# Cluster attention and two expert layers on one core: fp32r transposes of queries, keys and third weights, first loads on two queues, the last output chunk in halves

## The chip, the cores and the metric

The kernel runs on one core of a Trainium2 chip. TensorE (PE, with its weight loads, PEld), VectorE (DVE), ScalarE (ACT) and GpSimd (POOL) each run their own instructions in order and wait for each other by semaphores; SyncE (SP) issues most of the DMAs. The metric is device microseconds of one execution. Before the change the median of three runs is 740.92 us (740.73 to 741.88).

## The reference

```python
B, H, S, D = 2, 8, 768, 64          # 16 heads in all, 16 centroids a head
q_assign = argmax(q_n . c_n)         # each query and key goes to its nearest centroid
k_assign = argmax(k_n . c_n)
scores = q @ k.T / 8, -1e9 where q_assign != k_assign
x = softmax(scores) @ v              # to 1536 tokens x 512
x = ((x @ w1) * (x @ w2)) @ w3 @ w_out          # w1, w2: 512x1024; w3: 1024x1024; w_out: 1024x512
h = x @ w_in2                                   # 512x2048
out = (h * clip(h + 3, 0, 6) / 6) @ w_out2      # 2048x512
```

The weights of the two expert layers come as 64-bit floats and are read as pairs of 32-bit words.

## The kernel before, in words

**Order.** Every piece of work is an `op` with a key, an engine, the keys it needs and the buffer rings it takes and drops. `Plan.order` (L333) sorts the ops by the table `RANK`, which holds one place in the whole program for each op, and picks the engine of an op with a choice from the strings in `ON`. The ops are then emitted in that order, and each engine runs its own in that order. Nothing is scheduled at run time.

**Attention, about the first 350 us.** For each of the 16 heads (`prep_ops`, L684) SP loads the queries and keys side by side into `qkn`, 128 tokens x 6 chunks x 128 columns (`load_qk`, L581, each a 192 KB DMA). PE transposes the six 128x128 chunks in two groups of three (`qk_T`, L605, tile `ptqk`), against the fp32 identity `id_f`. ACT writes the rounded half `qkH`, DVE the remainder `qkL`; SP moves parts between partitions (`kk`). PE multiplies by the centroids (`pa`), nine steps on DVE and POOL (`oh0` to `oh8`) make codes of the nearest centroid, and these enter the scores as 16 extra rows. Then for each of six chunks: scores on PE (tile `pst`, L746), row maximum on DVE (tile `den`, L758), exponential on ACT (tile `p`, L780). PE transposes `p` in groups of four (tile `ptr`, L796), ACT and DVE split the result in two fp32r halves `ph` and `pl`, PE multiplies by the values (`av`, L820).

The transposes of `p` are already in fp32r. `p` is written as an fp32 tile; `p_raw` (L764) then takes a second tile `praw` of type fp32r in the same buffer, with a pad of eight columns more, and writes one column of the pad from the constant `three`. The transposes read the data through `praw` and wait for that small write.

**Weights, beside attention.** Each 512 KB piece of 64-bit weights is loaded to `raw` and turned into fp32 by five ops (`conv_ops`, L994): two on ACT (`cvt`, `cvs`), a clamp on POOL or DVE (L1008), two on DVE (L1017, L1021). The result is in `cvs`, a ring of three buffers. `w3` is transposed on PE in 16 groups of four (`w3_T`, L1037, tile `pt`), again against `id_f`, and multiplied by `w_out` (`psw`, L1068), so that the layer needs one product less per token.

**After attention**, PE runs the products of the first layer for the first batch (L1144) beside attention, then the rest (`psab`, `psx`), and then the second layer (`psh`, L1707, and `po`, L1751). At the very end each of six 128x512 chunks of the output is copied from PSUM by ACT (`out_copy`, L1756) and stored by SP (`out_store`, L1760).

**Start.** SP issues all first loads. ACT loads the table of the square root for the centroids (`root`), and later that of the exponential (`warm`). PE has four blocks of matmuls without use (`idle`, L530) between its first real work.

Of the kernel before, what the change touches and what calls it, by code (L numbers as in the profile page):

```python
# [1858 lines left out]
```

## Time and profile before

| | |
|---|---|
| median of three runs | 740.92 us |
| the profiled execution's own time | 741.47 us |
| its span, first to last instruction | 739.7 us |
| busy: PE, DVE, ACT, POOL | 719.0, 611.5, 546.8, 201.9 us |
| matmuls | 4143 |

The span is taken from the first to the last instruction of the profile. Busy time of PE counts overlapping matmuls once. The prediction reads PE from the times at which its matmuls start, since a matmul's own duration overlaps the next one.

### The profile page before, as it was taken

The numbers are of one execution on the slowest core, as the hardware profiler recorded it, in microseconds if no ns is written. First come the engines' busy times: TensorE is split into PE (matmuls) and PEld (weight loads), VectorE is DVE, ScalarE is ACT, GpSimd is POOL, SyncE is SP. The second block draws the span as 40 slices with busy tenths as digits, with TensorE's granted clock in tenths as the row PEclk, the third lists the DMA queues.
The fourth block names the chain that finished last, engine by engine and source line by source line (L and its number), as shares of the span: only waits on it lengthen the run. The fifth ranks groups of instructions, "written<-read, shape, count | busy, mean of one in ns | idle before, by whom it ended". The sixth has DMA issues, their size and how long they took to land. (4 is left out here: it accounts for less than half of the span.)

```text
span 739.7 us, 12102 instructions
## 1 busy us (share of the span) xinstructions
PE 719.0 (97%) x4143; PEld 661.4 (89%) x4143; DVE 611.5 (83%) x1060; ACT 546.8 (74%) x1043; POOL 201.9 (27%) x258
## 2 busy tenths in 40 slices
PE   5699999999999999999999999999999999999998
PEld 4488888888999999999999999999888998998986
DVE  6999999999899888778999999888897666666542
ACT  4899999898888878789867676676666656564543
POOL 3452646332635263355301110110110210011100
PEclk9999999999999999999999999999999999999999
DMA  8668555465563656453566752633222221411202
GB/s 237 157 167 221 152 150 162 114 161 140 150 185 119 182 155 170 115 156 114 178 200 228 238 175 100 220 122 138 91 86 85 72 72 60 137 61 58 72 28 86
DMA packets 81742, 101.97 MB, mean 138 GB/s; under 512 B 30960, under 2 KB 56592, under 8 KB 81680
## 3 DMA queue, kind: packets, MB, share of 16 engines
q1 hardware_dynamic: 81680, 101.20, 45.7%
q8 instruction: 33, 0.54, 0.3%
q14 instruction: 29, 0.24, 0.1%
HBM read 71.34 MB, written 15.78 MB: 118 GB/s over the span
## 5 line engine op out<-in xcount | busy, mean ns | idle before, releaser
L424 DVE TENSOR_TENSOR pl<-ptr,ph 128x512 fp32r<-128x512 f32 x144 | 96.3, 681 | 7.3 <-ACT ph L427 6.9
L758 DVE TENSOR_REDUCE den<-pst 128x1 f32<-128x768 f32 x96 | 91.1, 949 | 10.3 <-PE pst L746 9.2
L427 ACT ACTIVATE ph<-ptr 128x512 fp32r<-128x512 f32 x144 | 84.4, 597 | 14.0 <-PE ptr L796 9.7
L780 ACT ACTIVATE p<-pst,den 128x768 f32<-128x768 f32 x96 | 86.8, 904 | 8.8 <-DVE den L758 7.5
L1144 PE MATMUL psab<-xT,abhl 128*128 128x384 f32 x384 | 81.2, 343 | 0.6 <-DVE g L1154 0.6
L1008 POOL TENSOR_SCALAR cvt<-cvt 128x512 f32<-128x512 f32 x55 | 39.3, 718 | 142.0 <-ACT cvt L427 110.3
L746 PE MATMUL pst<-kk,qkL 128*128 128x512 f32 (+1 forms) x192 | 71.4, 374 | 4.8 <-ACT p L780 4.7
L1144 PEld LDWEIGHTS psab<-xT,abhl 128*128 128x128 f32 x384 | 65.4, 188 | 2.0 <-DVE g L1154 0.9
L820 PE MATMUL av<-ph,vs 128*128 128x384 f32 x192 | 66.4, 346 | 0.0
L796 PEld LDWEIGHTS ptr<-id_r,praw 128*128 128x128 f32 x576 | 60.9, 140 | 5.8 <-DVE pl L424 0.2
L746 PE MATMUL pst<-kk,qkH 128*128 128x512 f32 (+1 forms) x192 | 64.2, 338 | 1.7 <-ACT qkH L427 1.3
L820 PE MATMUL av<-pl,vs 128*128 128x384 f32 x192 | 64.8, 338 | 0.0
L427 ACT ACTIVATE m_sn<-psh 128x384 f32<-128x384 f32 x64 | 31.3, 489 | 44.3 <-PE psh L1707 43.4
L796 PE MATMUL ptr<-id_r,praw 128*128 128x128 f32 x576 | 63.6, 240 | 0.0
L427 ACT ACTIVATE cvt<-raw 128x512 f32<-128x512 f32 x72 | 48.1, 672 | 11.8 <-DVE cvs L1021 6.8
L1017 DVE SCALAR_TENSOR_TENSOR cvs<-cvt,cvs 128x512 int32<-128x512 int32 x72 | 50.0, 696 | 7.5 <-POOL cvt L1008 4.2
L1021 DVE SCALAR_TENSOR_TENSOR cvs<-cvt,cvs 128x512 int32<-128x512 int32 x72 | 50.8, 709 | 0.4
L427 ACT ACTIVATE cvs<-raw 128x512 int32<-128x512 uint8 x72 | 48.1, 670 | 1.8 <-DMA set<-cvs 1.8
L1068 PE MATMUL psw<-woh,wT 128*128 128x512 f32 x128 | 49.3, 405 | 0.0
L746 PEld LDWEIGHTS pst<-kk,qkL 128*128 128x128 f32 x192 | 36.0, 187 | 12.2 <-ACT p L780 9.9
L1751 PE MATMUL po<-m_whl,m_gv 128*128 128x512 f32 x162 | 44.0, 393 | 0.0
L1729 ACT ACTIVATE tt<-m_sn,three 128x384 f32<-128x384 f32 x48 | 29.4, 613 | 18.8 <-DVE m_sn L1717 9.0
(198 smaller groups left out, 1836.0 us busy)
## 6 DMA issues: line engine op xcount, KB each, us to landing
raw<-in_moe_w_dram SPq DMA_DIRECT2D x32, 512.0 KB, 4.3
m_gb<-set SPq DMA_DIRECT2D x64, 256.0 KB, 2.9
raw<-in_moe_w_out_dram SPq DMA_DIRECT2D x24, 512.0 KB, 3.4
raw<-in_moe_w_in_dram SPq DMA_DIRECT2D x16, 512.0 KB, 4.9
set<-cvs SPq DMA_DIRECT2D x32, 256.0 KB, 3.0
kk<-qkH SPq DMA_DIRECT2D x16, 384.0 KB, 4.0
abp<-cvs SPq DMA_DIRECT2D x16, 256.0 KB, 2.8
b_gv<-abp SPq DMA_DIRECT2D x16, 256.0 KB, 4.7
```

The costliest lines, as they stand in the source:

```text
L424: nc.vector.tensor_tensor(out=out, in0=a, in1=b, op=ALU.subtract)
L427: nc.scalar.activation(out=out, in_=in_, func=AF.Copy, **kw)
L746: x = mm(out=psr[:, t, ks_], lhsT=TT[nm, h][:, i, cs_], rhs=flat(TT["K", h][:, a])[:, ks_], start=st, stop=sp)
L758: done["mx", n] = [other_banks(nc.vector.tensor_reduce(out=den_at(h, 0, c), in_=psS[h, c], axis=AX.X, op=ALU.max, negate=True), ("S", n + 1))]
L780: done["ex", n] = [other_banks(nc.scalar.activation(out=p, in_=psS.pop((h, c)), func=AF.Exp, bias=den_at(h, 0, c), accum_out=den_at(h, 1, ...
L796: x = nc.tensor.transpose(pt[:, blk(j)], raw[h, hf][0][:, c, blk(kb)], id_r)
L820: mm(out=t[:, 0:HF], lhsT=vs_t[h][:, 2 * s + i, :], rhs=x_[:, c0:c0 + HF], start=(s == 0 and i == 0 and n == 0), stop=(s == 2 and i == 1 a ...
L1017: stt(out=s, in0=cvt[key], scalar=3, in1=s, op0=ALU.logical_shift_left, op1=ALU.bitwise_or)
L1021: stt(out=s, in0=cvt.pop(key), scalar=-0x80000000, in1=s, op0=ALU.bitwise_and, op1=ALU.bitwise_or)
L1068: mm(out=ps, lhsT=wT[m, hf][:, a, blk(kk)], rhs=w_[hf][:, kk, :], start=(kk == 0 and n == 0), stop=(kk == 3 and n == 2))
L1144: mm(out=ps[:, 0:HF], lhsT=s[:, w, a, blk(kk)], rhs=xT0[0][:, x_, kk, hf * HF:hf * HF + HF], start=(kk == 0 and n == 0), stop=(kk == KD - ...
L1751: mm(out=outs[b, c], lhsT=g[:, a, blk(c % 3)], rhs=w[:, w_, :], start=(first and a == 0 and w_ == 0), stop=(last and a == 1))
```

## The change

It does five things. (1) The centroids and the keys of head 0 are loaded from ACT's queue; the first DMA on SP's queue is now a weight piece. (2) The transposes of queries and keys of heads 1 to 15, and those of `w3`, go through fp32r tiles with a pad, as those of `p` did; a new op writes the pad (`tw` for each head, `ww` for each `w3` group) on ACT, POOL or DVE. (3) The ring tiles `qkn` and `cvs` become numbered buffers with eight more columns. (4) The last output chunk is copied in two halves, one on ACT and one on DVE, and stored in two halves, from ACT's and from SP's queue. (5) All numbers of `RANK` and many letters of `ON` are new.

```diff
-    "T": """
-        17 19 27 38 143 145 275 280 426 429 562 563 699 701 814 819 935 938 1062 1068 1180 1190 1317 1319 1451 1452 1579 1585 1717
+    "T": """
+        17 19 28 32 161 163 287 297 432 456 573 574 717 720 842 843 963 970 1090 1091 1214 1215 1338 1354 1476 1482 1564 1626 1743
...
+    "lk": "3 7 75 199 166 423 466 609 824 956 1008 1208 1380 1462 1611 1676",
+    "tw": "25 146 283 408 564 692 681 897 1009 1150 1307 1431 1521 1650 1774",
...
-    "pw": "dppdppppaaapppppapdaddpaadaadpdd",
+    "pw": "pddpddapdadppppappappdpppddddpad",
+    "tw": "addappppaaaapaa",
+    "ww": "pdpddadpppaadppp",
-    "c1": "ppppddpppppppppdppppppppppppppddpppppppppddpppddppppddpdpppppdppppdpdpdd",
+    "c1": "pdpppppppppppppppppppppppppddppppdpdppppppddpdddpdppdpddppdppddddpdpppdd",
...
     def cen_load():
         W_["cen"] = at.tile([128, D], F32, tag="p0", name="cen")
-        nc.sync.dma_start(out=W_["cen"], in_=centroids.rearrange("h c d -> (h c) d"))
+        nc.scalar.dma_start(out=W_["cen"], in_=centroids.rearrange("h c d -> (h c) d"))
...
+    def pad_write(e, pad):
+        if e == "act":
+            return nc.scalar.activation(out=pad, in_=three, func=AF.Copy)
+        return (nc.gpsimd if e == "pool" else nc.vector).tensor_copy(out=pad, in_=three)
+
     def load_qk(src, i, h):
         b, hh = divmod(h, H)
         if i == 0:
-            q_n[h] = ar.tile([128, NC, 2 * D], F32, tag="qkn", name="qkn", bufs=2)
-        nc.sync.dma_start(out=q_n[h][:, :, D * i:D * i + D], in_=src[b, hh].rearrange("(p c) d -> p c d", c=NC))
+            q_n[h] = ar.tile([128, S + 8], F32, tag=f"qkn{h % 2}", name="qkn")[:, 0:S].rearrange("p (c d) -> p c d", c=NC)
+        (nc.scalar if h + 1 == i else nc.sync).dma_start(out=q_n[h][:, :, D * i:D * i + D], in_=src[b, hh].rearrange("(p c) d -> p c d", c=NC))
...
+    def qk_raw(e, h):
+        del q_n[h]
+        x = ar.tile([128, S + 8], F32R, tag=f"qkn{h % 2}", name="qkr")
+        qraw[h] = x[:, 0:S].rearrange("p (c d) -> p c d", c=NC), pad_write(e, x[:, S:S + 1])
+
     def qk_T(h, hf):
+        if h:
+            x, w = qraw.pop(h) if hf else qraw[h]
+            pt = ps_s.tile([128, HF], F32R, tag="s", name="ptqk")
+            W_["st", h, hf] = pt.bitcast(F32)
+            for c in range(3):
+                i = nc.tensor.transpose(pt[:, blk(c)], x[:, 3 * hf + c, :], id_r)
+                tc.add_manual_dep(i.ins, w.ins.name, SYNC)
+            return
         pt = W_["st", h, hf] = ps_s.tile([128, HF], F32, tag="s", name="ptqk")
         for c in range(3):
             nc.tensor.transpose(pt[:, blk(c)], q_n[h][:, 3 * hf + c, :], id_f)
...
     def w3_T(m, hf):
-        pt = W_["pt", m, hf] = ps_s.tile([128, 4, 128], F32, tag="s", name="pt")
+        x, w = wraw.pop((m, hf))
+        pt = ps_s.tile([128, 4, 128], F32R, tag="s", name="pt")
+        W_["pt", m, hf] = pt.bitcast(F32)
         for i in range(4):
-            nc.tensor.transpose(pt[:, i, :], cvo["w3", m, hf][:, blk(i)], id_f)
-        cvo.pop(("w3", m, hf))
+            j = nc.tensor.transpose(pt[:, i, :], x[:, blk(i)], id_r)
+            tc.add_manual_dep(j.ins, w.ins.name, SYNC)
+        give("w3", m, hf)
...
-        copy_act(t, outs[b, c], scale=1.0 / 6.0)
+        copy_act(t[:, 0:half_of(b, c)], outs[b, c][:, 0:half_of(b, c)], scale=1.0 / 6.0)
+
+    def half_of(b, c):
+        return 256 if (b, c) == (1, 2) else 512
+
+    def last_copy(b, c):
+        copy_on("dve", W_["osb", b, c][:, 256:512], outs[b, c][:, 256:512], scale=1.0 / 6.0)
+
+    def last_store(b, c, i):
+        r = slice(256 * i, 256 * i + 256)
+        (nc.sync if i else nc.scalar).dma_start(out=out[b * S:(b + 1) * S, :].rearrange("(p c) n -> p c n", c=NC)[:, c, r],
+                                                in_=W_["osb", b, c][:, r])
```

What moves at the start, on PE: the program's first rows before. `ptqk` are the transposes of queries and keys (three for half a head), `pc` that of the centroids, `pa` the products with the centroids (four a head), `idle` the matmuls without use, `pt` the transposes of `w3`.

```order
L608 MATMUL ptqk<-id_f,qkn 128x128 x6
L556 MATMUL pc<-id_r,cs 128x128 x2
L608 MATMUL ptqk<-id_f,qkn 128x128 x3
L647 MATMUL pa<-qkH,cT 128x384
L647 MATMUL pa<-qkL,cT 128x384
...
L608 MATMUL ptqk<-id_f,qkn 128x128 x3
L534 MATMUL idle<-id_r 128x512 x4
L1040 MATMUL pt<-id_f,cvs 128x128 x4
L534 MATMUL idle<-id_r 128x512 x4
```

And the same stretch in the changed program:

```order
L634 MATMUL ptqk<-id_f,qkn 128x128 x6
L562 MATMUL pc<-id_r,cs 128x128 x2
L629 MATMUL ptqk<-id_r,qkr 128x128 x6
L675 MATMUL pa<-qkH,cT 128x384
L675 MATMUL pa<-qkL,cT 128x384
...
L540 MATMUL idle<-id_r 128x512 x8
L1084 MATMUL pt<-id_r,cvr 128x128 x4
```

Both halves of head 1 (`qkr`) now stand ahead of the first `pa` of head 0; before, the second half stood behind it. The eight `pa` of heads 0 and 1 follow each other, and the eight `idle` too.

On ACT, the first rows before:

```order
L506 ACT_TABLE_LOAD
L506 ACTIVATE warm<-three 128x1
L528 ACTIVATE cst<-cst 128x1
L427 ACTIVATE cvt<-raw 128x512
L427 ACTIVATE cvs<-raw 128x512
L615 ACTIVATE qkH<-ptqk,qks 128x384 x3
```

And in the changed program:

```order
L523 DMA cen<-in_centroids_dram 128x64
L596 DMA qkn<-in_k_dram 128x6x64
L512 ACT_TABLE_LOAD
L512 ACTIVATE warm<-three 128x1
L534 ACTIVATE cst<-cst 128x1
L433 ACTIVATE cvt<-raw 128x512
L433 ACTIVATE cvs<-raw 128x512
L643 ACTIVATE qkH<-ptqk,qks 128x384 x2
L512 ACT_TABLE_LOAD
L512 ACTIVATE warm<-three 128x1
L589 ACTIVATE qkr<-three 128x1
L643 ACTIVATE qkH<-ptqk,qks 128x384 x2
```

Two DMA issues now stand at the head, and the second table load and the pad write of head 1 stand between the `qkH` of head 0 and those of head 1; before, the second table load stood right ahead of the first exponential but one instruction.

On DVE, between the row maxima (`den`) of the first and second chunk of head 0, before:

```order
L758 TENSOR_REDUCE den<-pst 128x1
L665 TENSOR_REDUCE as_292<-as_291 128x12
L1017 SCALAR_TENSOR_TENSOR cvs<-cvt,cvs 128x512
L667 TENSOR_TENSOR as_291<-as_291,as_292 128x192
L1021 SCALAR_TENSOR_TENSOR cvs<-cvt,cvs 128x512
L758 TENSOR_REDUCE den<-pst 128x1
```

And in the changed program:

```order
L788 TENSOR_REDUCE den<-pst 128x1
L1042 TENSOR_SCALAR cvt<-cvt 128x512
L693 TENSOR_REDUCE as_276<-as_275 128x12
L1052 SCALAR_TENSOR_TENSOR cvs<-cvt,cvs 128x512
L695 TENSOR_TENSOR as_275<-as_275,as_276 128x192
L1056 SCALAR_TENSOR_TENSOR cvs<-cvt,cvs 128x512
L788 TENSOR_REDUCE den<-pst 128x1
```

One clamp of a weight piece (L1042), which POOL ran before, now stands in front of the other four.

## Rows read from the trace of the kernel before

**Rows 1.** Busy us by stretch (PE, PEld, DVE, ACT, POOL), clock, DMA share, GB/s.
```profile
40.00:200.00 160.00, 159.59 (x1017) 140.53 (x1016) 153.87 (x261) 146.14 (x294) 75.17 (x107) 1.00 0.58 154
200.00:350.00 150.00, 149.59 (x993) 143.02 (x992) 129.26 (x219) 128.02 (x260) 66.40 (x76) 1.00 0.53 152
350.00:500.00 150.00, 149.15 (x850) 146.87 (x849) 139.43 (x238) 106.75 (x188) 19.40 (x19) 1.00 0.57 184
```

**Rows 2.** Waits of PE's matmuls, 0 to 40 us: total, times, longest.
```profile
PE ptqk L608 <- DMA qkn<-in_k_dram: 8.0, 1, 8.0
PE pst L746 <- ACT p L780: 4.4, 4, 2.3
```

**Rows 3.** The same, 40 to 350 us.
```profile
PE pst L746 <- DMA qkH<-cd: 0.4, 1, 0.4
PE pst L746 <- ACT p L780: 0.3, 1, 0.3
```

**Rows 4.** PE in order of time (start, us, line, out<-in, count): fp32 transposes.
```profile
45.64 0.60 PE L1040 MATMUL pt<-id_f,cvs 128*128 128x128 f32 x4
46.00 0.54 PE L796 MATMUL ptr<-id_r,praw 128*128 128x128 f32 x4
...
117.80 0.82 PE L608 MATMUL ptqk<-id_f,qkn 128*128 128x128 f32 x6
118.37 0.48 PE L1068 MATMUL psw<-woh,wT 128*128 128x512 f32 x1
```

**Rows 5.** The same view, fp32r transposes.
```profile
47.84 0.45 PE L796 MATMUL ptr<-id_r,praw 128*128 128x128 f32 x4
48.13 0.47 PE L746 MATMUL pst<-kk,qkL 128*128 128x512 f32 x1
...
111.58 0.80 PE L796 MATMUL ptr<-id_r,praw 128*128 128x128 f32 x8
112.22 0.46 PE L1068 MATMUL psw<-woh,wT 128*128 128x512 f32 x1
```

**Rows 6.** Small writes to the pad of `praw`: count, duration ns min/median/max.
```profile
L771 DVE CAST praw<-three x9: 111/154/154, 30.1 to 341.9; 128x1 fp32r<-128x1 f32 x9
L769 ACT ACTIVATE praw<-three x9: 187/203/218, 111.1 to 300.6; 128x1 fp32r<-128x1 f32 x9
```

**Rows 7.** The clamp on DVE, same columns.
```profile
L1008 DVE TENSOR_SCALAR cvt<-cvt x17: 412/421/2071, 68.4 to 541.4; 128x512 f32<-128x512 f32 x17
```

**Rows 8.** SP's queue in order of time, first DMA issues: start, us.
```profile
0.74 1.37 SPq L585 DMA_DIRECT2D qkn<-in_q_dram  x2
...
2.83 0.43 SPq L989 DMA_DIRECT2D raw<-in_moe_w_dram  x1
3.30 0.55 SPq L585 DMA_DIRECT2D qkn<-in_k_dram  x1
```

**Rows 9.** DMA throughput in 40 slices of 0.5 us, 0 to 20 us.
```profile
GB/s 0 0 0 0 94 221 227 230 242 353 321 267 286 319 304 255 266 301 401 410 336 188 90 80 250 178 227 197 203 240 221 248 385 344 393 393 280 165 180 222
```

**Rows 10.** PE, ACT, DVE in order of time, start of head 0; brackets: idle before.
```profile
11.65 0.66 PE L647 MATMUL pa<-qkH,cT 128*128 128x384 f32 x1 [1.02 <-DVE cT L562]
...
8.87 1.22 ACT L615 ACTIVATE qkH<-ptqk,qks 128x384 fp32r<-128x384 f32 x2 [0.56 <-PE ptqk L608]
...
21.81 1.28 ACT L506 ACT_TABLE_LOAD   x1
...
23.76 0.89 ACT L780 ACTIVATE p<-pst,den 128x768 f32<-128x768 f32 x1
...
23.96 0.69 DVE L1017 SCALAR_TENSOR_TENSOR cvs<-cvt,cvs 128x512 int32<-128x512 int32 x1 [1.20 <-ACT cvs L427]
```

**Rows 11.** The page, part 5: copies of 512 and 384 columns from PSUM on ACT.
```profile
L427 ACT ACTIVATE osb<-po 128x512 f32<-128x512 f32 x12 | 6.8, 591 | 5.0 <-PE po L1751 5.0
...
L427 ACT ACTIVATE m_sn<-psh 128x384 f32<-128x384 f32 x64 | 31.3, 489 | 44.3 <-PE psh L1707 43.4
```

**Rows 12.** Waits of SP's queue: total us, times, longest.
```profile
SPq L989 <- ACT cvs L427: 84.8, 37, 9.6
```

More of the change, by code (lines that the diff above doesn't have):

```diff
@@ L215 @@
+    "abg": "1312 1400 1526 1547 1670 1716 1780 1834 1887 1952 2035 2099 2177 2214 2156 2299",
+    "xdone": "2246",
+    "Wh": "2138 2157 2170 2194",
+    "Wl": "2143 2166 2182 2207",
+    "top": "2233",
+    "gsh": "2237 2241 2245 2251 2265 2284 2267 2313",
+    "gsl": "2242 2249 2253 2257 2282 2294 2329 2342",
+    "x2": """
[5 rows of a table added]
+        2947 2950 2952""",
[6 rows of a table added]
     "bsm": """
-        2243 2283 2298 2315 2355 2367 2378 2390 2401 2412 2420 2422 2455 2457 2460 2461 2513 2530 2531 2537 2577 2581 2600 2618 2620
@@ L310 @@
+    "oc2": "3560 3568 3584 3599 3573 3621 4017 4015 4032 4018 4028 4026",
+    "os2": "3563 3793 3789 3787 3589 3670 4019 4023 4035 4021 4030 4029",
+    "oc3": "4033",
+    "os3": "4034",
 }
 ON = {
[L313 to L321 removed]
+    "Ck": "aa",
@@ L322 @@
+    "Cq": "da",
+    "pw": "pddpddapdadppppappappdpppddddpad",
+    "tw": "addappppaaaapaa",
+    "oh1": "dppppppppppppdd",
+    "oh4": "pppppppppdpddpp",
+    "xh": "appp",
+    "c1": "pdpppppppppppppppppppppppppddppppdpdppppppddpdddpdppdpddppdppddddpdpppdd",
+    "woh": "papppppp",
+    "ww": "pdpddadpppaadppp",
+    "Wl": "pddp",
     "gsl": "dddddddd",
@@ L325 @@
     "g1s": "dddd",
-    "Ll": "dddddddddpdddddddpdddddpddpdddpd",
-    "wol2": "dddpdpddddddddppdpddddddpdddddpd",
-    "xwl": "dddddddddddddp",
-    "xs": "dpddpddp",
+    "Ll": "dddddddddpddddppdddddddddpddpddd",
+    "wol2": "ddddddddddddddpddppdddddddpddpdp",
+    "xwl": "pdddddddddpddd",
+    "xs": "ddddddpd",
 }
@@ L562, in cen_C @@
         nc.vector.tensor_copy(cTv[r, :, c:c + 2 * NCL].rearrange("p h (s c) -> p s h c", s=2), W_["pc"][r])
-    op("cenl", "dma", 0.3, cen_load, due=-11.85, lat=2.0, take=("p",))
+    op("cenl", "act", 0.6, cen_load, due=-11.85, lat=2.0, take=("p",))
     op("cen1", "dve", 0.6, cen_1, ("cenl",), due=-14, take=("as1",))
@@ L608, in qk_T @@
             nc.tensor.transpose(pt[:, blk(c)], q_n[h][:, 3 * hf + c, :], id_f)
+        if hf:
+            del q_n[h]
     def qk_hi(h, hf):
@@ L687, in prep_ops @@
         SB = {"p": 0.96, "d": 0.47}
-        op(("lq", h), "dma", 0.7, lambda: load_qk(q, 0, h), due=b - 12, lat=2.0, take=("qn",))
-        op(("lk", h), "dma", 0.7, lambda: load_qk(k, 1, h), [("lq", h)], due=b - 11.9, lat=2.0)
+        op(("lq", h), "dma", 0.7, lambda: load_qk(q, 0, h), due=b - 12, lat=2.0, take=("qn",), after=[("T", h - 2, 1)] * (h > 1))
+        op(("lk", h), "dma" if h else "act", 0.7, lambda: load_qk(k, 1, h), [("lq", h)], due=b - 11.9, lat=2.0)
         op(("lv", h), "dma", 0.7, lambda: load_v(h), due=b - 5, lat=2.0, take=("vn",))
@@ L692, in prep_ops @@
         fop("s", ("vlo", h), SB if h >= WHOLE else {"p": 0.3}, lambda e: v_lo(e, h), (("vhi", h),), due=b - 1.9, drop=("vn",))
+        if h:
+            fop("tw", ("tw", h), {"a": 0.25, "p": 0.12, "d": 0.08}, lambda e: qk_raw(e, h), [("lq", h), ("lk", h)], due=b - 7, lock=False)
         for hf in range(2):
             dd = b - 6.5 + 0.4 * hf
-            op(("T", h, hf), "pe", 0.22, lambda hf=hf: qk_T(h, hf), [("lq", h), ("lk", h)], due=dd, take=("s",),
-               drop=("qn",) if hf else (), after=[("T", h, 0)] * hf)
+            op(("T", h, hf), "pe", 0.22, lambda hf=hf: qk_T(h, hf), [("tw", h)] if h else [("lq", h), ("lk", h)], due=dd, take=("s",),
+               drop=("qn",) if hf else (), after=[("T",) + divmod(2 * h + hf - 1, 2)] * (h + hf > 0))
             op(("qkh", h, hf), "act", 0.375, lambda hf=hf: qk_hi(h, hf), [("T", h, hf)] + [("qkh", h, 0)] * hf, due=dd + 0.05,
@@ L992, in cluster_attention_moe_kernel, with give @@
     ts, stt = nc.vector.tensor_scalar, nc.vector.scalar_tensor_tensor
+    slots, held = list(range(3)), {}
+    def give(*key):
+        slots.append(held.pop(key))
     def conv_ops(key, src, k_, due, big=None):
@@ L1011, in c_low @@
         def c_low(e):
-            s = cvo[key] = base.tile([128, 512], I32, tag="cvs", name="cvs", bufs=3)
+            held[key] = slots.pop(0)
+            s = cvo[key] = base.tile([128, 520], I32, tag=f"cvs{held[key]}", name="cvs")[:, 0:512]
             copy_act(s, raws.pop(key).bitcast(U8)[:, :, 3], scale=1.0 / 32.0, bias=-15.5 / 32.0)
@@ L1060, in wo_lo @@
         sub_on(e, wol[g // 4][:, g % 4, :], cvo.pop(("wo", g)), woh[g // 4][:, g % 4, :])
+        give("wo", g)
     def w_mm(m, g):
@@ L1130, in ab_lo @@
         sub_on(e, abs_[j][:, w, 1], cvo.pop(("ab", j, w)), abs_[j][:, w, 0])
+        give("ab", j, w)
     def ab_store(j, w):
@@ L1592, in set_store @@
         nc.sync.dma_start(out=set_dram[j][:, w], in_=cvo.pop(("set", j, w)))
+        give("set", j, w)
     for j in range(J2):
```

214 lines of the change are left out of this document (105 added, 109 removed), and 254 rows, old and new, of the table RANK.

## Prediction

> **What bounds the kernel.** I read the busy time by stretch first. From 40 to 350 us PE is busy for 309.2 of 310 us, from 350 to 500 for 149.2 of 150 [rows 1]. Busy time can hide waits, since matmuls overlap, so the waits come next: between 40 and 350 us PE waited 0.7 us for other engines in all [rows 3]; 12.4 us lie ahead of 40 us: 8.0 until the first key is there and 4.4 for the exponentials of head 0 [rows 2]. So there are two kernels in one. For the first 35 us or so PE waits for a chain of DMA, ACT and DVE. From there to the end PE's own instruction stream is the time, and work taken from PE is worth its full length, as long as the next engine has room. The next one is DVE: 153.9 of 160 us busy between 40 and 200, 129.3 of 150 and 139.4 of 150 after that [rows 1]. The reader should see that DVE's room is 6 us in the tightest stretch, more than this change asks of it there.
>
> **Transposes in fp32r.** A matmul's duration overlaps the next one, so a group of transposes costs the time from its first start to the start of what follows. Four fp32 transposes of `w3` take 46.00 - 45.64 = 0.36 us, six of queries and keys 118.37 - 117.80 = 0.57 us [rows 4]. Four fp32r transposes of `p` take 48.13 - 47.84 = 0.29 us, eight take 112.22 - 111.58 = 0.64 us [rows 5]. The shapes are the same and the stationary operand is the data in both, so I take these as the new prices.
> - `w3`: 16 groups of four, each 0.36 - 0.29 = 0.07 us less: 1.1 us.
> - Queries and keys, heads 1 to 15 (head 0 stays fp32): six fp32r transposes lie between four and eight, (0.29 + 0.64) / 2 = 0.465 us, so 0.10 us less a head, 1.5 us for fifteen. In both orders eight of the sixteen heads run in two groups of three, apart, where less lies inside a group; by that the gain may be near nothing. Between 0 and 1.5 us I take the middle, 0.75 us, an estimate.
>
> Together 1.85 us, called 1.8, with 1.1 and 2.6 as ends. All of it lies on PE's stream, which is the bound.
>
> **What the pads and the moved work cost.** By the program's order ACT gets 11 new pad writes and loses four of `praw`: 7 x 0.20 = 1.4 us. DVE gets 7 new ones and three more of `praw`: 10 x 0.15 = 1.5 us [rows 6]. Five more clamps run on DVE: 5 x 0.42 = 2.1 us [rows 7], and five small steps of the codes move there from POOL, at most a clamp's price each, again 2.1 us. That is 5.7 us of DVE's time over the whole program, most of it after 200 us, where DVE has 20.7 us of idle time up to 350 and 10.6 up to 500 [rows 1]; the clamps of the `w3` pieces go to POOL instead. PE covers it; I price it at nothing. If that cover is gone, the price is up to 5.7 us, less what DVE has of room.
>
> **The start.** Four steps.
> 1. *Loads.* Today the key of head 0 is the fifth issue on SP, at 3.30 us, behind two query loads, the centroids and 512 KB of weights, which were issued from 0.74 to 2.83 [rows 8]; it is there at about 7.96, where PE's wait of 8.0 ends [rows 2]. Bytes move from 2.0 us on, at about 225 GB/s while the query loads move and at 353 with the weights [rows 9]. By these rates the load would be done at 2.0 + 416 KB / 225 + 512 KB / 353 + 192 KB / 225 = 6.2 us; it took 1.8 more. In the changed order centroids and key stand on ACT's queue, and the query stands behind the weights on SP's: 512 KB / 353 + 416 KB / 225 = 3.3 us, done at 5.3, and with the same 1.8 at 7.1 us. So the first transposes start some 0.9 us earlier. The two ends are 0 (the query behind 512 KB gives it back) and 1.9 us (the difference in the time of issue alone).
> 2. *Centroid products.* They started at 11.65 us [rows 10]. Now PE has all six transposes of head 1 ahead of them, which wait for a pad write on ACT, which stands behind the exponential's table load. From 7.1: 0.9 us until `qkH` (8.87 - 7.96), 1.22 for the pair, 1.28 for the table [rows 10], two small ACT instructions of 0.2 [rows 6], and about 0.9 for the transposes: 11.8 us. The 0.9 us won is spent again.
> 3. *First exponential.* It started at 23.76, behind the table load at 21.81, and DVE stood idle for 1.20 us at the same time, for an ACT instruction behind that load [rows 10]. The load is gone from here: 1.28 us won. DVE's clamp (0.42) and a pad write (0.15) now stand between its row maxima: 0.57 lost. Net 0.7 us.
> 4. *Idle matmuls.* As many as before; they fill waits.
>
> So 0.7 us for the start, with ends of -0.5 (the key of head 1 late, ACT held at its pad) and 1.9.
>
> The Trainium skill has a rule against this part ("DMA: Bandwidth & Descriptors", Issuing engines are not separate DMA queues): all issuing engines feed the same 16 DMA engines, and using several saves only the issue time. By it the second queue moves no byte sooner; the start would give nothing and the sum below would be 2.0 us. No row here shows two queues at once.
>
> **The end.** The last copy of 512 columns takes 0.591 us, one of 384 takes 0.489 [rows 11]: 0.8 ns a column, so 256 columns take 0.39 us. Two halves on two engines are ready 0.2 us earlier, and half a store is no longer than a whole one. I take 0.2, with ends 0 and 0.6.
>
> **The order.** Moving ops cannot win much between 40 and 350 us, where PE waited 0.7 us in all [rows 3]; it can lose. I take nothing.
>
> **Sum.** 1.8 + 0.7 + 0.2 = 2.7 us off the profiled execution's 741.47: 738.8. The median of the three runs is 0.55 below that execution, so the forecast is 738.2 us. What measurement can tell from no change is 0.2%, 1.5 us: under 739.4 is faster, over 742.4 slower.
>
> **Rivals.**
> - *The start gives more.* Step 2 is wrong, the chain of head 0 runs 1.9 us earlier, the transposes save 2.6 and the end 0.4: 741.47 - 4.9 - 0.55 = 736.0. For it: 12.4 us of waits lie there [rows 2]. Against: the table load stands in the way.
> - *The start gives nothing*, since the first query now waits behind 512 KB: 1.8 + 0.2 = 2.0 off, 738.9 us. For it: bytes moved all the time from 2.0 us on [rows 9]. It is also what the skill's rule would make of it.
> - *DVE becomes the bound.* It is 96% busy from 40 to 200 us [rows 1], and if ACT and DVE set the pace there, a shorter PE stream only waits. Only start and end count: 0.9 off, 740.0 us. Against: PE's waits of 0.7 us [rows 3]; something that waits this little is not paced by others.
> - *Slower: a pad holds an engine.* A pad write waits until both loads of its head are there, and on ACT it stands in a row in front of the exponentials. Before, only PE waited for these loads. SP's queue runs late at times: it waited 84.8 us in all, up to 9.6, for buffers of the weight pieces [rows 12]. If a load is issued that late, ACT stands until it lands (the first key took 4.7 us from issue), then DVE and PE. It decides from the second such pad on: two of 4.5 us each, 9.0 - 2.7 = 6.3 us more, 747.2 us. Against: between 40 and 350 us PE never waited for a query or key load [rows 3], and in the new table (`lk`, `tw` in the diff) the pad writes of heads 2 to 15 stand 39 to 242 places behind the key's load.
>
> **Chances.** Forecast 0.40 (its own range 737.2 to 739.2), more at the start 0.20, nothing at the start 0.15, DVE 0.15, pads 0.10. Faster: nearly all of the first two, and 0.12 of the third: 0.70. Same: the DVE case and the rest: 0.20. Slower: 0.10. The range leaves out the pads and the last tenth below: 735.6 to 740.6 us.
>
> **What would show it.** Right: groups of four `pt` from first start to the next at 0.29 us, and six `ptqk` under 0.5; PE's waits from 40 to 350 us still about 1 us; first transposes near 7.1 us, first centroid product near 11.8, first exponential near 23.0; the last copy under 0.45 us. Wrong: PE's matmuls waiting for DVE or ACT between 40 and 350 us by some us (DVE's case), ACT or POOL idle ahead of `qkr` for a DMA (pads), or a first transpose at 8 us or later (nothing at the start). A time under 736 would mean that the first 40 us lost far more of their waits than I gave them.

## The result, and the profile after

The changed kernel takes 747.88 us (median of 6 runs), the kernel before 741.45 us in the same runs: 1.0093 times as long, with an interval of 1.0076 to 1.011. It is 6.4 us slower by the medians and 6.9 by the ratio, where some 3 us less had been forecast, and outside the range. (The ratios here and below leave disturbed runs out; where a median of all runs and the ratio differ, the ratio is used.)

The profiled execution has a span of 746.2 us. The waits of PE's matmuls in it, with the total, the number and the longest:

```profile
PE ptqk L634 <- DMA qkn<-in_q_dram: 6.6, 1, 6.6
PE pst L776 <- ACT p L810: 4.2, 4, 1.6
PE po L1800 <- DVE m_hl L430: 2.9, 1, 2.9
PE av L850 <- DVE pl L430: 2.6, 2, 1.8
PE ptqk L629 <- ACT qkr L589: 2.1, 1, 2.1
...
PE psh L1756 <- DVE m_sn L1766: 0.9, 1, 0.9
```

The first two lines answer to [rows 2]: 10.8 us where there were 12.4. The line of `qkr` is new and lies at the start: it is the pad of head 1. Behind 40 us three more of these lines are new, and all three name DVE: `po` waits for `m_hl` (the expert's second layer), `av` for `pl` (attention), `psh` for `m_sn` (the expert's first layer). Two of these places lie behind 500 us, in a stretch of which the prediction read neither waits nor busy time. The busy time by stretch (PE, weight loads, DVE, ACT, POOL), answering to [rows 1], and one stretch more:

```profile
40.00:200.00 160.00, 158.33 (x1022) 139.60 (x1021) 154.27 (x267) 144.69 (x298) 80.17 (x117) 1.00 0.59 152
200.00:350.00 150.00, 149.74 (x994) 142.41 (x993) 133.63 (x227) 129.41 (x261) 62.17 (x71) 1.00 0.52 149
350.00:500.00 150.00, 147.70 (x829) 145.12 (x827) 138.91 (x241) 103.46 (x182) 14.74 (x16) 1.00 0.57 188
500.00:600.00 100.00, 96.26 (x481) 86.50 (x480) 78.43 (x130) 61.69 (x113) 12.91 (x7) 1.00 0.23 75
```

The last of these stretches in the kernel before:

```profile
500.00:600.00 100.00, 99.89 (x500) 89.95 (x499) 79.79 (x138) 63.64 (x117) 13.16 (x9) 1.00 0.27 90
```

PE's share has gone down most behind 350 us, and there DVE is no fuller than before: from 500 to 600 us it is busy for 78 us of 100, and before it was 80. So it isn't that DVE has no room.

To see where the time went without trusting busy time, I took for every matmul the time from its start to the next start, less the usual spacing of its form (0.231 us for 512 columns, 0.174 for 384, 0.119 for 256; transposes 0.109 in fp32 and 0.067 in fp32r, the last of a group 0.029 and 0.086). What is left I call PE's idle time. It holds small variations of the spacing too (19.5 us from 40 to 350 us before, where PE waited 0.7), so its differences count. By stretch:

| us | before | changed | four letters moved (below) |
|---|---|---|---|
| start of the first transposes | 7.96 | 6.64 | 6.42 |
| sum of the usual spacings | 691.7 | 689.1 | 689.1 |
| idle, to 40 us | 13.8 | 14.7 | 15.6 |
| idle, 40 to 350 us | 19.5 | 20.8 | 20.0 |
| idle, 350 to 500 us | 1.7 | 5.2 | 3.2 |
| idle, 500 to 600 us | 0.7 | 4.8 | 1.4 |
| idle, 600 us to the last matmul | 0.3 | 0.9 | 0.9 |
| start of the last matmul | 735.6 | 742.2 | 736.5 |

Against before, the change wins 2.6 us on the transposes and 1.3 on the first load, and loses 10.4 us to idle time, 7.6 of it between 350 and 600 us.

Two of the places, in order of time (start, us, engine, line, form). At 347 us:

```profile
347.36 3.49 DVE L1052 SCALAR_TENSOR_TENSOR cvs<-cvt,cvs 128x512 int32<-128x512 int32 x2
...
347.74 2.56 POOL L427 TENSOR_TENSOR Whl<-W,Whl 128x1024 fp32r<-128x1024 f32 x1 [1.47 <-ACT Whl L433]
```

The usual length of such a step on DVE stands in the view of one tile (shortest, median, longest, in ns):

```profile
L1052 DVE SCALAR_TENSOR_TENSOR cvs<-cvt,cvs x72: 627/682/2883, 7.6 to 537.3; 128x512 int32<-128x512 int32 x72
```

Of the two steps at 347.36 one is the 2.88 us. POOL's subtraction ends at 347.74 + 2.56 = 350.30 us, DVE's second step at 347.36 + 3.49 = 350.85. So the step sat there until POOL was done, and only then took about its usual time. `pl`, for which PE waits, stands behind it on DVE. At 573 us the same thing happens twice in a row:

```profile
573.33 3.15 POOL L427 TENSOR_TENSOR m_gB<-m_gb,m_gB 128x1280 fp32r<-128x1280 f32 x1 [15.99 <-ACT m_gB L433]
...
573.51 0.87 PE L1800 MATMUL po<-m_w,m_whl 128*128 128x512 f32 x3
573.61 3.70 DVE L430 TENSOR_TENSOR x2f<-x2f 128x768 f32<-128x768 f32 x1
...
576.46 1.97 POOL L427 TENSOR_TENSOR m_w<-m_gb,m_w 128x512 fp32r<-128x512 f32 x1
577.23 1.74 DVE L430 TENSOR_TENSOR m_hl<-m_gb,m_hl 128x512 fp32r<-128x512 f32 x1
578.90 0.95 DVE L430 TENSOR_TENSOR m_whl<-x2f,m_whl 128x768 fp32r<-128x768 f32 x1
...
579.03 0.73 PE L1800 MATMUL po<-m_hl,m_gv 128*128 128x512 f32 x2 [2.87 <-DVE m_hl L430]
```

A step of 128x768 takes DVE 0.95 us (the line at 578.90); at 573.61 it took 3.70, ending 0.83 us after POOL's. `m_hl` started late behind it, met POOL's next instruction and took 1.74 us, where one at 572.67 took 0.68. PE waited 2.87 us. The kernel before has such meetings too, and PE does not wait for what they delay (same view; behind 350 us PE waits 0.8 us in all there):

```profile
665.16 3.22 POOL L421 TENSOR_TENSOR m_gB<-m_gb,m_gB 128x1280 fp32r<-128x1280 f32 x1 [4.59 <-ACT m_gB L427]
...
665.77 3.02 DVE L1733 SCALAR_TENSOR_TENSOR tt<-tt,m_sn 128x384 f32<-128x384 f32 x1 [0.22 <-ACT tt L1729]
```

How many such meetings there are does not decide. I counted the DVE instructions that took over 0.25 us more than the median of their operation and shape; each of them has a POOL instruction beside it. Before the change there are 14, which are 10.9 us over in sum, and in the changed kernel 17, which are 15.5 us over.

**Theory T**: the code of the change gives about what was forecast; the new order and engine letters put long POOL instructions beside DVE ones for whose result PE waits, and a DVE instruction that meets one is held until POOL is done. **Rivals**: R1, the code itself costs (pads, loads); R2, the order leaves too little room between producer and consumer, or POOL's results come too late; R3, DVE has too much to do.

### The profile page after: what moved, and what is told of

The parts are those of the page before. It is cut to its first block, busy times and chain, and to the rows that moved or that the text cites. A ratio compares the mean times of both kernels' runs of the same rounds, so it can differ in the third digit from the quotient of the medians.

```text
span 746.2 us, 12124 instructions
## 1 busy us (share of the span) xinstructions
PE 719.2 (96%) x4143; PEld 659.1 (88%) x4143; DVE 619.5 (83%) x1083; ACT 545.4 (73%) x1048; POOL 199.0 (27%) x262
## 4 chain that ended last, share of the span: by engine, by line
PE 50%; DVE 9%; ACT 2%; issue 2%; POOL 0%; DVEq 0%; ACTq 0%
PE po L1800 16%; PE psh L1756 14%; PE psx L1307 6%; PE psab L1192 4%; PE psab L1444 4%; PE av L850 2%; PE pst L776 2%; PE ptr L826 1%; DVE x2f L430 1%; DVE cvs L1052 1%; DVE m_gb L1663 1%; DVE cvs L1056 1%; DVE b_sn L1453 1%; DVE b_gv L1418 0%; ACT cvt L433 0%
## 5 line engine op out<-in xcount | busy, mean ns | idle before, releaser
L433 ACT ACTIVATE ph<-ptr 128x512 fp32r<-128x512 f32 x144 | 84.0, 598 | 10.6 <-PE ptr L826 7.2
L1042 POOL TENSOR_SCALAR cvt<-cvt 128x512 f32<-128x512 f32 x50 | 35.3, 708 | 125.8 <-ACT cvt L433 64.9
L1052 DVE SCALAR_TENSOR_TENSOR cvs<-cvt,cvs 128x512 int32<-128x512 int32 x72 | 53.5, 745 | 0.1
L1114 PE MATMUL psw<-woh,wT 128*128 128x512 f32 x128 | 51.0, 410 | 0.0
L1056 DVE SCALAR_TENSOR_TENSOR cvs<-cvt,cvs 128x512 int32<-128x512 int32 x72 | 49.5, 688 | 0.4
L776 PEld LDWEIGHTS pst<-kk,qkL 128*128 128x128 f32 x192 | 35.9, 187 | 13.5 <-ACT p L810 10.9
L1778 ACT ACTIVATE tt<-m_sn,three 128x384 f32<-128x384 f32 x48 | 29.2, 612 | 21.0 <-DVE m_sn L1766 10.8
L1800 PE MATMUL po<-m_hl,m_gv 128*128 128x512 f32 x144 | 39.5, 395 | 2.9 <-DVE m_hl L430 2.9
```

The source lines that it names most:

```text
L433: nc.scalar.activation(out=out, in_=in_, func=AF.Copy, **kw)
L776: x = mm(out=psr[:, t, ks_], lhsT=TT[nm, h][:, i, cs_], rhs=flat(TT["K", h][:, a])[:, ks_], start=st, stop=sp)
L1052: stt(out=s, in0=cvt[key], scalar=3, in1=s, op0=ALU.logical_shift_left, op1=ALU.bitwise_or)
L1056: stt(out=s, in0=cvt.pop(key), scalar=-0x80000000, in1=s, op0=ALU.bitwise_and, op1=ALU.bitwise_or)
L1800: mm(out=outs[b, c], lhsT=g[:, a, blk(c % 3)], rhs=w[:, w_, :], start=(first and a == 0 and w_ == 0), stop=(last and a == 1))
```

## The experiments

The kernels ran in three groups, each on one chip with the kernel before (741.05, 741.51 and 741.12 us).

### The old order with the new code

All of the change's code in the order and letters of before; each new pad write is put right ahead of its transposes.

```diff
-    "tw": "25 146 283 408 564 692 681 897 1009 1150 1307 1431 1521 1650 1774",
+    "tw": "27 146 279 435 574 714 831 955 1085 1204 1343 1478 1607 1746 1883",
...
```

(the places of the pads of heads 1 to 15, in a table whose other rows are those of before, moved on by the new steps; the loads of the query of head 5 and of query and key of head 12 stand later than before.)

> All code of the change (loads on ScalarE's queue, fp32r transposes with their pads, last chunk in halves), in the old order with the old engine letters; only the new pads, the two moved issues and the fp32r steps are put where they have to stand. Theory T (the code gains about what was forecast, the new order loses it by putting long POOL instructions beside DVE ones where PE has no slack): 741.5 - 2.6 (transposes, as the first starts in the new trace add up) - 0.2 (end) - 0 to 1 (start) = 737.7 to 738.7 us. Rival R1 (the code itself costs: pads on ACT and DVE, loads in the way): 741 us or more.

Measured: 754.47 us, 1.0178 times before (1.0161 to 1.0194). With the transposes alone:

```diff
-        (nc.scalar if h + 1 == i else nc.sync).dma_start(out=q_n[h][:, :, D * i:D * i + D], in_=src[b, hh].rearrange("(p c) d -> p c d", c=NC))
+        nc.sync.dma_start(out=q_n[h][:, :, D * i:D * i + D], in_=src[b, hh].rearrange("(p c) d -> p c d", c=NC))
...
-        return 256 if (b, c) == (1, 2) else 512
+        return 512
...
```

> Old order and letters, all loads on SP, last chunk whole; only the transposes of queries, keys and third weights are fp32r, with their pad writes. Theory T: 741.5 - 2.6 = 738.9 us, or a little more if not all of the shortened stream comes through. Rival R1 (the pads cost what the transposes save, or more): 741.5 us or more.

Measured: 754.82 us, 1.0176 times before (1.0162 to 1.0189). Both are misses for T, and R1 seems to hold. But PE's waits in the first of them say which cost it is:

```profile
PE ptqk L482 <- ACT qkr L442: 6.2, 7, 3.1
PE pt L937 <- DVE cvr L443: 5.2, 5, 2.7
PE ptqk L487 <- DMA qkn<-in_k_dram: 5.2, 1, 5.2
PE ptqk L482 <- POOL qkr L443: 2.9, 3, 1.7
```

`qkr` and `cvr` are the tiles that the pads write. With three more lines of 1.0 to 1.1 us PE waits 17.5 us for pads (the later expectation, which says 18.6, counted one line too many). A pad of 0.15 to 0.20 us [rows 6] made PE wait up to three us where it stands one place ahead of its reader; that its engine is then in the middle of other work is my reading. So these two kernels test my placing, and not the change: there PE waits 2.1 us for one pad. The repair is to place most of the pads 20 to 30 steps earlier (that of head 1 only two, and four of the weights' pads two to eleven):

```diff
-    "tw": "27 146 279 435 574 714 831 955 1085 1204 1343 1478 1607 1746 1883",
+    "tw": "25 120 249 405 544 683 801 927 1055 1174 1313 1448 1577 1716 1853",
...
-    "tw": "addappppaaaapaa",
+    "tw": "dddappppaaaapaa",
...
```

> As the run with all code of the change in the old order, but each new pad write now stands 20 to 30 steps ahead of its transposes (behind its loads) instead of right ahead of them; the first pad of head 1 and that of one weight piece go on DVE. Theory T2 (the 13 us lost there were PE waiting for pads that stood behind other work of their engine, 18.6 us of waits for pads by the waits of PE): those waits go, and what is left is the gain of the code, 741.1 - 2.6 - 0.2 - 0 to 1 = 737 to 738.5 us. Rival R1 (the pads cost by what they take from their engines, wherever they stand): 745 us or more.

> The same with the loads back on SP and the last chunk whole: old order, only the transposes in fp32r with early pads. Theory T2: 741.1 - 2.6 = 738.5 us, up to 739.5. Rival R1: 745 us or more. The difference to the run beside it is what the loads and the halves of the end give: 0.2 to 1.2 us by the forecast.

Measured: 745.28 us, 1.0045 times before (1.0031 to 1.0059), and with the transposes alone 745.96 us, 1.006 (1.0046 to 1.0074). 9.9 and 8.6 of the 13 us are back, so most of it was the place of the pads; the forecast of 737 to 739.5 is missed all the same, and the 745 or more of the rival R1 is met. Most of what is left lies at the start: by the table's method idle time to 40 us is 20.2 us in the first of these, against 13.8 before, though the first transposes start 2.8 us earlier; from 40 to 350 us it is 21.3 against 19.5, and from 350 us on 4.0 against 2.7. The largest new wait is for a pad:

```profile
PE ptqk L482 <- DVE qkr L443: 3.6, 1, 3.6
```

This one, of head 1, I had given to DVE, where it was written at 10.35 us behind a step on the weights and the first remainder of head 0. Another engine for it was not tried in this order. The two kernels differ by 0.0015, 1.1 us: that is what loads and halved end give here, and it is no larger than its uncertainty (1.5).

### The old order behind 358 us

The changed kernel up to its first `x2` step, and behind it the order and the letters of before:

```diff
...
-    "Ll": "dddddddddpddddppdddddddddpddpddd",
+    "Ll": "dddddddddpdddddddpdddddpddpdddpd",
...
-    "xs": "ddddddpd",
+    "xs": "dpddpddp",
```

> The changed kernel's order and letters up to its first x2 step (about 358 us), the old order and letters for all that comes after. Theory T: the waits after 358 us go (about 1.4 us between 400 and 500, 4.1 between 500 and 600, 0.6 after that, by the starts of the matmuls against the old trace), the one at 350 us stays: 747.9 - 6 = 742 us, 741 to 743.5. Rival R1 (the code costs, wherever the order comes from): 747 to 748 us.

Measured: 742.13 us, 1.0011 times before (0.9997 to 1.0025). Nearly all of the loss is gone with the order behind 358 us, and all the code of the change is in place. So R1 falls as a reason for the 6.4 us; that the code gives its 2.7 us is not shown by it. Counted as above this kernel has 16 meetings of 14.7 us, nearly the sum of the changed one: what counts is whether PE waits for the step that is held.

### Four letters

Order, code and all else as in the changed kernel; four steps go from POOL to DVE:

```diff
-    "Wl": "pddp",
+    "Wl": "pddd",
-    "Ll": "dddddddddpddddppdddddddddpddpddd",
+    "Ll": "dddddddddpdddddddddddddddpddpddd",
-    "xs": "ddddddpd",
+    "xs": "dddddddd",
```

> The changed kernel in its own order; only four letters differ: the split of third weight piece 3, the two halves of the last LayerNorm product of group 7 and one x2 step of batch 1 go from POOL to DVE. These are the long POOL instructions that ran beside a DVE instruction several times its usual length in the new trace. Theory T: though DVE gets 4.3 us more to do, the waits of PE at 350 (1.9 us), 558 (0.9) and 575 to 579 us (2.9) go: 747.9 - 4 to 6 = 742 to 744 us. Rival R2 (the order leaves too little room between producer and consumer, whatever POOL does) and R3 (DVE has too much to do): 748 us, or up to 4 us more.

Measured: 742.02 us, 1.0015 times before (1.0005 to 1.0025): nearly all of the loss against the kernel before is undone by four letters, in a program of some 4,000 steps. The last column of the table above is this kernel's: of the 10.4 us of idle time that the change had added, 5.3 are gone and 5.1 remain, 1.8 of them ahead of 40 us. What the transposes and the first load win (2.6 and 1.5 us) pays for most of the rest. R3 falls with it, since DVE has four instructions more; what DVE's busy time did is read off the pages, of the changed kernel first and then of this one:

```profile
PE 719.2 (96%) x4143; PEld 659.1 (88%) x4143; DVE 619.5 (83%) x1083; ACT 545.4 (73%) x1048; POOL 199.0 (27%) x262
```

```profile
PE 721.3 (97%) x4143; PEld 661.2 (89%) x4143; DVE 614.9 (83%) x1087; ACT 545.3 (74%) x1048; POOL 189.8 (26%) x258
```

Four instructions more, which take 1.22 + 1.49 + 0.69 + 0.95 = 4.35 us on DVE where nothing meets them, and 4.6 us less of busy time: some 9 us of DVE's busy time in the changed kernel was no work. R2 is still open here, since with the letters POOL's results are gone as well.

### POOL busy for nothing

The kernel with the four letters, and at each of the four places POOL does something whose result nobody reads. In one it subtracts the same inputs into a scratch tile, in the other it fills the tile with zeros for about as long:

```diff
+    dum = const.tile([128, 816], mybir.dt.bfloat16, name="dum")
+
+    def extra(a, b):
+        n, k = a.shape[1], a.shape[2]
+        m = 768 // k
+        for r in range(0, n, m):
+            sub_pool(dum[:, 0:min(m, n - r) * k].rearrange("p (n k) -> p n k", k=k), a[:, r:min(r + m, n)], b[:, r:min(r + m, n)])
...
```

```diff
...
+        sub_pool(dum[:, 0:1], a[:, 0, 0:1], b[:, 0, 0:1])
+        for r in range(0, n, m):
+            for _ in range(3):
+                nc.gpsimd.memset(dum[:, 0:min(m, n - r) * k], 0.0)
...
```

> The kernel with the four letters moved to DVE; in addition POOL runs at each of these four places subtractions of about the same size on the same inputs, whose result goes to a scratch tile that nobody reads. So POOL is as busy there as in the changed kernel, but no other engine waits for what it makes. Theory T (a POOL instruction that reads SBUF holds up the DVE instruction beside it): DVE instructions at about 347, 555 and 573 us take two to four times their usual length again, PE waits there again: 744 to 748 us. Rival R2 (the four letters helped because PE, ACT or DVE no longer waited for POOL's results, or through the order alone): 742 us, and DVE's instructions there have their usual length.

> The same, but in place of the subtractions POOL only fills the scratch tile with zeros, in several instructions that together last about as long, behind one subtraction of a single column that waits for the same inputs. Nothing is read from SBUF while it fills. If what holds DVE up is POOL's reading: 742 us, as without the extra work, and DVE's instructions there have their usual length. If any work of POOL does it: as the run beside it.

Measured: with the subtractions 749.88 us, 1.0108 times before (1.0093 to 1.0122); with the fills 741.57 us, 1.0 times before (0.9992 to 1.0009). The place at 347 us, with subtractions (POOL and DVE, in order of time):

```profile
346.72 2.39 DVE L913 SCALAR_TENSOR_TENSOR cvs<-cvt,cvs 128x512 int32<-128x512 int32 x2
...
347.09 3.17 POOL L288 TENSOR_TENSOR dum<-W,Whl 128x512 bf16<-128x512 f32 x2 [1.46 <-ACT Whl L294]
...
349.04 1.77 DVE L917 SCALAR_TENSOR_TENSOR cvs<-cvt,cvs 128x512 int32<-128x512 int32 x1
...
350.84 0.69 DVE L291 TENSOR_TENSOR pl<-ptr,ph 128x512 fp32r<-128x512 f32 x1
```

and with fills:

```profile
346.52 1.29 DVE L915 SCALAR_TENSOR_TENSOR cvs<-cvt,cvs 128x512 int32<-128x512 int32 x2
...
347.32 3.44 POOL L287 MEMSET dum<- 128x512 bf16 x6
...
347.73 0.69 DVE L919 SCALAR_TENSOR_TENSOR cvs<-cvt,cvs 128x512 int32<-128x512 int32 x1
348.45 0.69 DVE L293 TENSOR_TENSOR pl<-ptr,ph 128x512 fp32r<-128x512 f32 x1
```

The three steps on `cvs` take 1.29 + 0.69 us beside the fills and 2.39 + 1.77 beside the subtractions, and `pl` comes 2.4 us later. PE's waits with the subtractions are those of the changed kernel again, and somewhat more:

```profile
PE av L711 <- DVE pl L291: 3.8, 2, 3.0
PE psh L1623 <- DVE m_sn L1633: 2.6, 2, 2.0
...
PE po L1667 <- DVE m_hl L291: 1.8, 1, 1.8
```

Nobody reads the scratch tile, so R2's late results can't be it, and with the fills the same order loses nothing, so it has the room: R2 falls. The subtractions also keep their inputs' buffers in use for longer, but a wait for a buffer shows as idle time ahead of an instruction, and here the instructions themselves are longer. Nor is it that POOL is busy. POOL reading from SBUF is what holds DVE, and 6.9 us hang on these four places (the difference of the ratio to that of the four letters, 0.0093; to that of the fills, in the same group, it is 0.0108, 8.0 us).

The fills differ in one thing more: they are short, 0.52 to 0.74 us each. But a long POOL subtraction does not hold every DVE instruction either. In the kernel with the four letters, at 106 us:

```profile
106.71 1.40 POOL L280 TENSOR_TENSOR wol<-cvs,woh 128x512 fp32r<-128x512 f32 x1
...
106.87 0.69 DVE L283 TENSOR_TENSOR pl<-ptr,ph 128x512 fp32r<-128x512 f32 x1
```

`pl` has one input from SBUF (`ph`) and one from PSUM (`ptr`), and takes its usual 0.69 us. In the traces of the kernel before and of the changed one 60 `pl` and 63 `den` (its one input is in PSUM) begin while a POOL operation on two tensors has over 0.3 us to go, and none is longer than usual. Of nine steps on `cvs`, with two inputs from SBUF, eight are, and so are all four on `tt<-tt,m_sn`.

The Trainium skill has this as a rule ("SBUF — State Buffer", SBUF: two separate sides): DVE and GpSimd (POOL here) have one pair of SBUF ports in common, which is locked for a whole instruction, and the other engine stands until it is free; on DVE's side that concerns instructions in a two-port mode, or, against a POOL instruction that reads SBUF, those with two inputs from SBUF. The runs agree: beside POOL's subtraction `x2f` (two SBUF inputs) took 3.70 instead of 0.95 us, beside the fills at 347, 547 and 571 us no DVE instruction was longer than usual.

### What the parts are worth

On top of the kernel with the four letters, one part of the change is undone at a time. First the transposes (the pads stay):

```diff
-                i = nc.tensor.transpose(pt[:, blk(c)], x[:, 3 * hf + c, :], id_r)
+                i = nc.tensor.transpose(pt[:, blk(c)], x[:, 3 * hf + c, :].bitcast(F32), id_f)
-            j = nc.tensor.transpose(pt[:, i, :], x[:, blk(i)], id_r)
+            j = nc.tensor.transpose(pt[:, i, :], x[:, blk(i)].bitcast(F32), id_f)
```

> The kernel with the four letters moved to DVE (742.0 us), but the transposes of queries, keys (heads 1 to 15) and third weights run in fp32 again; pads, order and loads stay. If the transposes give what the starts in the traces add up to: 742.0 + 2.6 = 744.6 us. By the forecast's 1.8: 743.8. If PE has slack for them: 742.

Measured: 743.9 us, 1.0038 times before (1.0024 to 1.0051). The difference of the two ratios, 0.0023, is 1.7 us, with about 1.2 of uncertainty from the two intervals. Then the loads:

```diff
-        nc.scalar.dma_start(out=W_["cen"], in_=centroids.rearrange("h c d -> (h c) d"))
+        nc.sync.dma_start(out=W_["cen"], in_=centroids.rearrange("h c d -> (h c) d"))
-        (nc.scalar if h + 1 == i else nc.sync).dma_start(out=q_n[h][:, :, D * i:D * i + D], in_=src[b, hh].rearrange("(p c) d -> p c d", c=NC))
+        nc.sync.dma_start(out=q_n[h][:, :, D * i:D * i + D], in_=src[b, hh].rearrange("(p c) d -> p c d", c=NC))
```

> The kernel with the four letters moved to DVE (742.0 us), but first keys and centroids are issued from SP again, in the places that the order gives them: centroids, query, key, then the weights. By the forecast's step on the loads: key and query land at about the same time as with two queues or somewhat earlier, since the weights now stand behind them; what two queues give is the time of issue alone, 0 to 0.7 us: 741.5 to 742.7 us. If the second queue is what the start lives on: 743 us or more.

Measured: 744.49 us, 1.0046 times before (1.0032 to 1.006), so the second queue is worth 0.0031, or 2.3 us, in this order, with 1.3 of uncertainty; the expectation of 741.5 to 742.7 is missed. (It has the weights behind the loads; in this kernel the first weight piece is still issued ahead of them, at 0.74 us.) The first transposes wait for the key until 6.9 us instead of 6.4, but idle time to 40 us is 0.9 us shorter, so by 40 us nothing of it is left. The largest difference lies between 80 and 120 us, 6.5 us of idle time by the table's method against 3.7, and it goes back to a load of weights (ACT, then DVE):

```profile
104.45 0.66 ACT L286 ACTIVATE cvt<-raw 128x512 f32<-128x512 f32 x1 [1.70 <-DMA raw<-in_moe_w_out_dram]
...
105.63 0.69 DVE L283 TENSOR_TENSOR pl<-ptr,ph 128x512 fp32r<-128x512 f32 x1 [1.47 <-ACT ph L286]
```

ACT's `ph`, then DVE's `pl` and then PE, for 1.4 us, stand behind that wait. The changed kernel, with two queues, waits 0.99 us for the same load in its trace, and the one with the four letters not at all. So whether the queue makes this load late, or it varies from execution to execution, is not shown.

### The old order behind 358 us, with one letter and one pad

The kernel with the old order behind 358 us, and the letter of the one place of the four that is left in it; and the same with the pad of head 1 on POOL:

```diff
...
-    "Wl": "pddp",
+    "Wl": "pddd",
...
```

> The kernel with the changed order up to the first x2 step and the old one behind it (742.1 us), and one letter more: the split of third weight piece 3 goes from POOL to DVE. Theory T: PE's wait of 1.8 us at 350 us goes, DVE gets 1.2 us more: 742.1 - 1.3 to 1.8 = 740.3 to 740.8 us, level with the kernel before or just under it. Rival R3 (DVE is the bound there): 742 or more.

```diff
-    "tw": "addappppaaaapaa",
+    "tw": "pddappppaaaapaa",
```

> As the run beside it, and the pad of head 1 is written by POOL instead of ACT, where it stood behind the exponential's table load (PE waits 2.1 us for it at 8.5 us). If the start is paced by that wait: up to 1 us less than the run beside it. If the chain of head 0 through DVE and ACT paces it: no difference.

Measured: 1.0001 times before (0.9991 to 1.001) and 0.9983 times (0.9971 to 0.9995). The letter is worth 0.0010, 0.7 us, where 1.3 to 1.8 were expected, and the intervals with and without it overlap. The second kernel, 739.68 us by its median, is 1.3 us faster than the kernel before (0.4 to 2.1 by the interval) and some 8 faster than the changed one. Head 1's transposes waited 2.1 us for a pad that stood behind the exponential's table load on ACT; they now wait for POOL:

```profile
PE ptqk L482 <- POOL qkr L443: 0.2, 1, 0.2
```

How much of the 1.3 us between these two is the pad's is not shown: in their traces the idle time to 40 us differs by 0.3 us, and the first transposes start 0.5 us earlier in the second, for a load that the pad does not touch.

## Why the prediction was wrong

**The step that failed** is "The order": "Moving ops cannot win much ... it can lose. I take nothing." It was the largest term of all: 10.4 us of idle time, 7.6 of them between 350 and 600 us. The kernel's order of work had been searched anew, and the two places shown from it were read for what stands ahead of what on one engine. Which POOL instruction runs beside which DVE instruction was not asked. The rows held a hint: the clamp with a median of 421 ns and a longest of 2071 [rows 7]. I took the median as its price and passed over the longest. That one, at 541.4 us, is a clamp beside a POOL subtraction.

The step before it rests on the same gap: "PE covers it; I price it at nothing" of 5.7 us more on DVE. DVE's busy time went from 611.5 to 619.5 us, but the loss doesn't come from the work moved there: the kernel with four more steps on DVE is the faster one. What failed is the cover. Room of 20.7 and 10.6 us by stretch [rows 1] is an average; `m_hl` had no room at 577 us, in a stretch where DVE is 78% busy.

No rival had the mechanism. "Slower: a pad holds an engine" came nearest in time (747.2) and was not it: PE waited for one of the new pads, 2.1 us, and for no load of a later head. "DVE becomes the bound" would have been 740. What can be said for the pads' rival is that pads do cost when they stand too near their readers (13 us in the first two experiments), only the changed order does not put them there.

Theory T's first half, that the code gives about what was forecast, is shown only in part: the transposes give 1.7 us with 1.2 of uncertainty, the end nothing, and the best kernel with all of the code is 1.3 us faster than before, where 2.7 had been forecast.

**What was right or nearly so**, by the prediction's own list:
- *Transposes* (1.8 us forecast, 1.7 measured by undoing them, 2.6 by the sum of spacings). Groups of four and six in the changed kernel, first start to the next, answering to [rows 4]:

```profile
44.81 0.46 PE L1084 MATMUL pt<-id_r,cvr 128*128 128x128 f32 x4
45.11 0.47 PE L1114 MATMUL psw<-woh,wT 128*128 128x512 f32 x1
...
117.12 0.63 PE L629 MATMUL ptqk<-id_r,qkr 128*128 128x128 f32 x6
117.58 0.47 PE L1114 MATMUL psw<-woh,wT 128*128 128x512 f32 x1
```

0.30 and 0.46 us, forecast 0.29 and 0.465. Groups of three, for which the forecast feared near nothing, take 0.21 us where most took 0.24 to 0.27.
- *First transposes*, forecast near 7.1 us, start at 6.64; the first centroid product, forecast near 11.8, at 11.23; the wait between them is the pad behind the table load, as step 2 had it:

```profile
6.64 1.51 PE L634 MATMUL ptqk<-id_f,qkn 128*128 128x128 f32 x6 [6.64 <-DMA qkn<-in_q_dram]
...
10.44 1.00 PE L629 MATMUL ptqk<-id_r,qkr 128*128 128x128 f32 x6 [2.07 <-ACT qkr L589]
11.23 0.65 PE L675 MATMUL pa<-qkH,cT 128*128 128x384 f32 x1
```

- *First exponential*, forecast near 23.0: 21.54 us, 2.2 earlier than before [rows 10]. Less of it stays than that, since idle time to 40 us is 0.9 us longer; the start as a whole gives 1.3 - 0.9 = 0.4 us by 40 us, against 0.7 forecast. The prediction had cited the Trainium skill ("DMA: Bandwidth & Descriptors", Issuing engines are not separate DMA queues), by which a second issuing engine saves only the time of issue. With the loads back on SP the first transposes start 0.5 us later, which agrees; the 2.3 us of the whole are more than that, and the trace leads them to a late load of weights at 104 us, of which it is open whether the queue brings it.
- *The end* (0.2 forecast) gives nothing. The last copy is indeed 0.39 us, but the two halves don't run side by side, though the sum took them so:

```profile
742.63 0.39 ACT L433 ACTIVATE osb<-po 128x256 f32<-128x256 f32 x1 [1.05 <-issue]
743.04 0.37 ACTq L1817 DMA_DIRECT2D out_dram<-osb  x1
743.05 0.42 DVE L476 TENSOR_SCALAR osb<-po 128x256 f32<-128x256 f32 x1 [7.00 <-ACT osb L433]
743.50 0.33 SPq L1817 DMA_DIRECT2D out_dram<-osb  x1
```

DVE's half starts when ACT's is done: the profile puts its wait down to ACT's copy, and the program names that copy among what the half needs (`oc2`, L1884). So the last store is issued 0.87 us after the first copy's start, where a whole copy took 0.60. From the copy's start to the end of the span it is 746.2 - 742.63 = 3.6 us, and before it was 739.7 - 736.10 = 3.6. The halves alone were not tried as a kernel.

The list of what would show it wrong asked for PE's waits from 40 to 350 us. They are 1.5 us there (`pl`, twice) against 0.7, and by the table PE's idle time is only 1.3 us longer; most of the loss came behind 350 us, where the prediction looked for no waits because PE had been full.

## What to carry to other kernels

When a change writes a new order or new engine assignments, look for the pairs it makes: a long POOL instruction that reads SBUF beside a DVE instruction with two inputs from SBUF, whose result TensorE needs next. In these traces nearly every such pair delayed DVE by what was left of POOL's instruction, while DVE instructions with an input from PSUM were not held. Busy shares don't show these pairs; a longest duration of several times the median, in the view of one tile or line, does. And a step that costs 0.2 us by itself (a pad) cost up to three here when it was placed right ahead of its reader.

## What the runs showed that was not expected

- A DVE instruction with two inputs from SBUF that meets a POOL subtraction stands until POOL is done and ends 0.3 to 0.8 us later, which is a little less than its usual length: 3.70 us for `x2f` (usually 0.95), 2.88 for a step on `cvs` (0.68), 1.74 for `m_hl` (0.69). POOL is held in its turn: `m_w` of 128x512 took 1.97 us beside `x2f`, where subtractions of 128x512 on POOL take 1.3 as a rule. The one clamp on DVE that met a subtraction, with a single input, was held too (2.07 us instead of 0.42, before the change). POOL's fills of 0.52 and 0.74 us beside the same DVE instructions cost these nothing.
- DVE's busy time counts the standing: with four more instructions it fell from 619.5 to 614.9 us.
- The last copy, split over ACT and DVE, ran in series, 0.39 and 0.42 us one after the other, as the program's own needs have it; two halves without that need were not tried.
